# Warm matmuls moved and added between the transposes, kv and x steps of the first batch

## Chip, cores, metric

One core of a Trainium2 chip. The metric is the time of one execution on the device in microseconds. Executions of one kernel lie up to some 2 us apart here, so medians and means over several are compared, and, where it matters, single executions by the TensorE clock that each of them lists.

## The reference

Linear attention over 8 batches, 8 heads, 576 rows of 64, then a feed-forward layer with exact Gelu, all float32 at the border:

```python
q_s = softmax(q, axis=-1)            # over the 64 of a row
k_s = softmax(k, axis=2)             # over the 576 rows
kv  = einsum('bhsd,bhse->bhde', k_s, v)
x   = einsum('bhsd,bhde->bhse', q_s, kv)   # then heads joined: 4608 x 512
h   = x @ w_in                       # 512 -> 2048
out = gelu(h) @ w_out                # 2048 -> 512
```

## The kernel before

The kernel treats each batch (512 of its 576 rows) as transposes of q, kv, x, h and y; the rests of all batches come last. Matmul operands are bf16. While the first data come in, TensorE (PE in the profile) runs matmuls on zeros, so that its clock is up when real work starts: in the trace of this kernel their starts lie 0.43 us apart until the clock comes up at 3.98 us, then 0.216 us, and the first transposes start at 9.33. These are called warm matmuls here.

```python
def warm(n):
    ps = psum_y.tile([128, DM], FP32, tag="y")
    for i in range(n):
        nc.tensor.matmul(ps, zeros[:, 0:128], zeros, start=True, stop=True)
...
setup_tiles()
warm(27)
table(AF.Exp)
exp_q(0, parts=2)
exp_k(0, parts=2)
norm_q(0, 0, 2)                       # POOL
norm_q(0, 1, 2, nc.vector)
tp_mm(0, 0)                           # 8 transposes
tp_evac(0, 0, "s")
table(AF.Gelu)
warm(2)
cast_v(0, 0)
for hp in range(1, HP):
    cast_v(0, hp, nc.gpsimd)
cast_wi(0, wi[0], "p")
cast_wi(1, wi[1], "p")
tp_mm(0, 1)                           # 8 transposes
for hp, pool, tag in ((0, psum_y, "y"), (1, psum_y, "y"), (2, psum_a, "a"), (3, psum_h, "h")):
    x_tile(0, hp, pool, tag)
kv_mm(0, 0)
kv_norm(0, 0, 1)                      # DVE
tp_evac(0, 1)
x_mm(0, 0)
...
h_phase(0, {0: [lambda: cast_wi(2, wi[2], "v")],   # third block of w_in, cast in 4 row blocks
            2: [lambda: cast_wi(3, wi[3], "v")],
            ...}, groups={0: 2})
```

In `h_phase` the tiles of h are computed one after another (tiles 0 and 1 interleaved), four matmuls each, one per row block of w_in. The third block of w_in holds tiles 4 to 7.

The softmax here doesn't subtract the row's maximum and nothing guards it: scores larger than these inputs give would overflow.

## Time and profile before

| | before |
|---|---|
| time, first three executions | 283.36, 283.38, 284.02 us |
| profiled execution | 283.92 us (span 282.1), listed clock 0.991 |
| PE busy | 97% of the span |
| half clock in the trace | 14.22 to 17.63 us, and after the last matmul |

The listed clock is the mean over the span. In this trace the stretch of 3.41 us at half clock takes 0.5 x 3.41 / 282 = 0.006 off it, and the idle end of the kernel, at half clock from 280.46 us, 0.003 more: 0.991. The clocks listed in this study fall into two groups, 0.988 to 0.993 and 0.997 or more (one execution at 0.853 aside); the two traces with a dip list 0.991, the nine without one and without a cold start 0.998 or more. So an execution that lists 0.997 or more is counted here as one without a dip inside, and one at 0.993 or less as one with.

### The profile page before, as it was taken

The page shows a single profiled execution, that of the slowest core. Times are in us where ns is not written, and L with a number is a line of the kernel's source. Part 1 is how long each engine was busy: PE and PEld are TensorE (multiplying, and loading weights), DVE is VectorE, ACT ScalarE, POOL GpSimd, SP SyncE. Part 2 cuts the span into 40 slices and gives each one's busy share as a digit, 9 for nine tenths or more (in the row PEclk, how much of TensorE's full clock was granted, in tenths as well). Part 3 has the DMA queues.
Part 4 walks back from the last instruction along what each step waited for, and adds up shares of the span by engine and source line. Part 5 has one row for each costly group of instructions (what it writes and reads, how often), then busy time and mean ns, then how long its engine had stood idle before and what let it go on. Part 6 is the DMA issues. An engine that isn't in the chain of part 4 may idle for free.

```text
span 282.1 us, 4576 instructions
## 1 busy us (share of the span) xinstructions
PE 273.1 (97%) x1933; PEld 126.3 (45%) x1933; DVE 101.8 (36%) x149; ACT 156.7 (56%) x242; POOL 32.8 (12%) x25
## 2 busy tenths in 40 slices
PE   8699999999999899999999999999999999999994
PEld 3334454444444344444444444444444444444443
DVE  2766586309760470075006510562006200230021
ACT  5756753689467914693468436862683364036400
POOL 0530040002020050005000500050005000000000
PEclk9979999999999999999999999999999999999998
DMA  7999999951629429911991179226601500120033
GB/s 233 382 404 428 401 402 406 401 223 55 136 83 349 163 80 249 379 41 39 221 369 47 74 198 346 89 77 164 136 0 74 149 2 0 74 77 0 2 74 74
DMA packets 44852, 50.09 MB, mean 178 GB/s; under 512 B 20385, under 2 KB 29857, under 8 KB 44577
## 3 DMA queue, kind: packets, MB, share of 16 engines
q1 hardware_dynamic: 44544, 49.68, 51.9%
q8 instruction: 15, 0.25, 0.4%
q10 hardware_dynamic: 288, 0.13, 0.2%
q14 instruction: 5, 0.03, 0.1%
HBM read 36.70 MB, written 9.44 MB: 164 GB/s over the span
## 4 chain that ended last, share of the span: by engine, by line
PE 84%; DMA 7%; DVE 3%; ACT 2%; SPq 1%; issue 1%; POOL 0%; ACTq 0%
PE ps L294 40%; PE ps L304 39%; DMA f<-in_v_dram 6%; PE kv L165 2%; PE ps L250 2%; DMA f<-in_q_dram 1%; PE ps L326 1%; DVE v_aug L144 1%; DVE qsum L195 1%; ACT ek L137 1%; ACT e L132 1%; DVE e L197 1%; SPq L230 0%; DVE y_sb L311 0%; ACT L132 0%
## 5 line engine op out<-in xcount | busy, mean ns | idle before, releaser
L294 PE MATMUL ps<-xT,wi_bf 128*128 128x512 bf16 x576 | 127.2, 382 | 0.0
L304 PE MATMUL ps<-wo_bf,g 128*128 128x512 bf16 x560 | 124.4, 379 | 1.3 <-DVE y_sb L311 1.3
L299 ACT ACTIVATE g<-ps 128x512 bf16<-128x512 f32 x144 | 85.6, 597 | 68.6 <-PE ps L294 68.6
L294 PEld LDWEIGHTS <-wi_bf 128*128 128x128 bf16 x576 | 56.6, 99 | 69.2 <-issue 1.9
L304 PEld LDWEIGHTS <-g 128*128 128x128 bf16 x560 | 54.0, 98 | 65.7 <-issue 2.0
L311 DVE COPY y_sb<-ps 128x512 f32<-128x512 f32 x35 | 23.8, 683 | 74.5 <-PE ps L304 74.1
L197 POOL TENSOR_TENSOR e<-e,recq 128x2048 bf16<-128x2048 bf16 (+1 forms) x9 | 25.7, 2855 | 179.1 <-DVE recq L196 146.9
L144 DVE CAST v_aug<-f 128x576 bf16<-128x576 f32 x26 | 17.9, 745 | 57.3 <-DMA f<-in_v_dram 57.2
L276 ACT CAST xT<-ps 128x512 bf16<-128x512 f32 x19 | 10.2, 588 | 31.9 <-PE ps L250 22.3
L195 DVE TENSOR_REDUCE qsum<-e 128x16 f32<-128x1024 bf16 (+1 forms) x13 | 21.0, 1618 | 15.6 <-ACT e L132 15.6
L132 ACT ACTIVATE e<-f 128x512 bf16<-128x512 f32 (+1 forms) x42 | 20.5, 556 | 1.2 <-DMA f<-in_q_dram 1.1
L137 ACT ACTIVATE ek<-f 128x2304 bf16<-128x2304 f32 (+1 forms) x10 | 17.2, 1730 | 2.4 <-DMA f<-in_k_dram 2.4
L274 DVE CAST xT<-ps 128x512 bf16<-128x512 f32 x15 | 9.7, 686 | 15.5 <-PE ps L250 12.7
L78 ACT ACT_TABLE_LOAD x9 | 11.5, 1283 | 2.8 <-issue 2.6
L404 PE MATMUL ps<-zeros 128*128 128x512 bf16 x29 | 8.0, 435 | 1.2 <-DVE scr L73 1.2
L132 ACT ACT_TABLE_LOAD x7 | 9.0, 1283 | 0.1
L165 PEld LDWEIGHTS <-ek 64*64 64x64 bf16 x576 | 6.6, 105 | 3.1 <-issue 1.2
L378 DVE CAST wi_bf<-w 128x512 bf16<-128x512 f32 (+1 forms) x8 | 7.1, 903 | 2.1 <-DMA w<-in_moe_w_in_dram 2.0
L165 PE MATMUL kv<-v_aug,ek 64*64 64x65 bf16 x576 | 7.1, 193 | 0.7 <-POOL v_aug L144 0.4
L397 DVE CAST wo_bf<-w 128x2048 bf16<-128x2048 f32 (+1 forms) x5 | 5.1, 1013 | 4.5 <-DMA w<-in_moe_w_out_dram 4.4
L197 DVE TENSOR_TENSOR e<-e,recq 128x1024 bf16<-128x1024 bf16 x4 | 6.3, 1586 | 0.1
L250 PE MATMUL ps<-qT,kvc 64*64 64x512 bf16 x60 | 5.2, 406 | 1.2 <-DVE kvc L176 1.2
(29 smaller groups left out, 40.5 us busy)
## 6 DMA issues: line engine op xcount, KB each, us to landing
out_dram<-y_sb SPq DMA_DIRECT2D x32, 256.0 KB, 2.3
f<-in_k_dram SPq DMA_DIRECT2D x6, 1152.0 KB, 10.0
f<-in_v_dram SPq DMA_DIRECT2D x6, 1152.0 KB, 11.6
f<-in_q_dram SPq DMA_DIRECT2D x6, 1024.0 KB, 7.5
w<-in_moe_w_in_dram SPq DMA_DIRECT2D x6, 512.0 KB, 8.4
f<-in_k_dram SPq DMA_DIRECT2D x4, 576.0 KB, 10.1
f<-in_v_dram SPq DMA_DIRECT2D x8, 288.0 KB, 8.1
f<-in_q_dram SPq DMA_DIRECT2D x4, 512.0 KB, 8.6
```

Source lines behind the costliest of these rows:

```text
L78: nc.scalar.activation(out=scr[:, 1:2], in_=scr[:, 0:1], func=func)
L132: nc.scalar.activation(out=dst[:, i], in_=src[:, u], func=AF.Exp)
L137: nc.scalar.activation(out=ek[b % 2][:, i:i + n], in_=st[b]["kf"][:, i:i + n].rearrange("p x (n d) -> p x n d", n=NS), func=AF.Exp,)
L144: eng.tensor_copy(out=v_aug[b % 2][:, hp, :, 0:D], in_=st[b]["vf"][:, hp, :].rearrange("p (n d) -> p n d", n=NS),)
L165: nc.tensor.matmul(ps[c, i, half, 0:D + 1], ek[b % 2][pr, hp, n, :], v_aug[b % 2][pr, hp, n, 0:D + 1], start=(n == 0), stop=(n == NS - 1),)
L195: nc.vector.reduce_sum(out=qsum, in_=eq[:, :, hs, :], axis=AX.X)
L197: eng.tensor_tensor(out=eq[:, :, hs, :], in0=eq[:, :, hs, :], in1=recq.unsqueeze(3).to_broadcast([128, J, w, D]), op=ALU.mult,)
L250: nc.tensor.matmul(ps[c, :], kvc[b][pr, hp, :], st[b]["qT"][pr, :, hp, :], start=True, stop=True,)
L294: nc.tensor.matmul(ps, wi_bf[:, dm, t * 128:(t + 1) * 128], xT[:, dm, :], start=(dm == 0), stop=(dm == NDM - 1),)
L299: nc.scalar.activation(out=g[:, t, :], in_=ps, func=AF.Gelu)
L304: nc.tensor.matmul(ps, st[c]["g"][:, t, j * 128:(j + 1) * 128], wo_bf[:, t, :], start=(t == 0), stop=(t == NDF - 1),)
L311: nc.vector.tensor_copy(out=y_sb, in_=ps)
```

## The change

Intent: to keep PE busy enough around the first kv and x step for the clock to stay up, without delaying them. Two warm matmuls move from the opening to behind the second transposes, and four new ones, on zeros, write the x tiles before x does.

```diff
+    def warm_x():
+        for r in range(2):
+            for i in range(2):
+                pr = slice(r * 64, r * 64 + 64)
+                c = slice((r ^ i) * 64, (r ^ i) * 64 + 64)
+                nc.tensor.matmul(
+                    st[0][f"x{i}"][c, :], zeros[pr, 0:64], zeros[pr, :], start=True, stop=True,
+                )
...
-    warm(27)
+    warm(25)
...
     tp_mm(0, 1)
+    warm(2)
     for hp, pool, tag in ((0, psum_y, "y"), ...
...
     tp_evac(0, 1)
+    warm_x()
     x_mm(0, 0)
```

## The prediction

The windows of the clock, here and below, are the stretches of 3.41 us that its steps mark in the traces: before the change it first comes up at 3.98 us, and its steps at 14.22, 17.63 and 280.46 us lie 3, 4 and 81 times 3.41 us after that.

> **What bounds the kernel now.** I read the page first, for which engine is full; then the windows view in small slices, for where TensorE's clock drops; then the chain of waits over the first 40 us, for what the changed code waits on; then the timeline of 8 to 20 us and of 42 to 47 us, for how early the later work could start.
>
> ```profile
> PE 273.1 (97%) x1933; PEld 126.3 (45%) x1933; DVE 101.8 (36%) x149; ACT 156.7 (56%) x242; POOL 32.8 (12%) x25
> ...
> PEclk9979999999999999999999999999999999999998
> DMA  7999999951629429911991179226601500120033
> ```
>
> TensorE (PE) is busy for 97% of the span, so after the start the kernel is a stream of matmuls. The third digit of PEclk, 14 to 21 us, shows a stretch at a lower clock. The DMA row shows that the transfers are full for the first 56 us. Both matter here. In slices of 0.1 us the clock reads 0.59 in 14.20:14.30 and 0.84 in 17.60:17.70, so it fell to half at 14.22 us and came back at 17.63 us: a dip of 3.41 us. The only other drop is at the end, in the slice 280.00:280.50 (0.96), so at 280.46. From 17.63 to 280.46 are 77.0 times 3.41, and counted back the same steps fall on 14.22, 10.81 and 7.39 us. I therefore cut the start into those stretches (columns: PE, PEld, DVE, ACT, POOL busy, clock, DMA share, GB/s):
>
> ```profile
> 7.39:10.81 3.42, 2.52 (x22) 1.21 (x21) 3.28 (x4) 2.25 (x3) 1.88 (x1) 1.00 1.01 377
> 10.81:14.22 3.41, 1.86 (x82) 1.19 (x79) 1.73 (x6) 3.28 (x6) 2.24 (x4) 1.00 1.08 392
> 14.22:17.63 3.41, 3.21 (x11) 1.12 (x12) 2.48 (x5) 0.84 (x2) 2.20 (x4) 0.50 1.06 402
> ...
> 277.05:280.46 3.41, 1.33 (x19) 1.03 (x17) 0.85 (x2) 0.00 (x0) 0.00 (x0) 1.00 0.55 135
> ```
>
> PE was busy for 74% of the first stretch and kept its clock. It was busy for 55% of the second and 39% of the last, and after each of those the clock was halved for the next stretch. The third stretch, at half clock, was full, and the clock came back. The bar lies, for this run, between 55% and 74%. The timeline shows where the holes of the second stretch are:
>
> ```profile
> 10.50 0.61 PE L211 MATMUL ps<-identity,e 128*128 128x128 bf16 x8
> ...
> 11.23 0.22 PE L165 MATMUL kv<-v_aug,ek 64*64 64x65 bf16 x2
> ...
> 11.88 0.47 PE L165 MATMUL kv<-v_aug,ek 64*64 64x65 bf16 x34 [0.43 <-POOL v_aug L144]
> ...
> 12.95 0.41 PE L250 MATMUL ps<-qT,kvc 64*64 64x512 bf16 x4 [0.60 <-DVE kvc L176]
> ...
> 14.42 0.64 PE L250 MATMUL ps<-qT,kvc 64*64 64x512 bf16 x4 [0.60 <-DVE kvc L176]
> ```
>
> The holes are 11.45 to 11.88 (the cast of v on POOL, itself waiting for v from DMA until 11.11), 12.35 to 12.95 and 13.85 to 14.42 (the normalisation on DVE). The change fills the first two.
>
> [...]
>
> **The change part by part.**
> 1. The opening burst goes from 27 to 25 matmuls. At full clock a 128x512 matmul takes 0.216 us (four per Gelu; their starts lie 0.86 us apart). So the burst ends at about 8.11 and not 8.54 us. The transposes wait for POOL until 9.33 either way: 0 us on the path. The stretch 7.39:10.81 loses 0.43 of its 2.52 us: 2.09, 61%.
> 2. Two such matmuls after the second transposes: 11.11 to 11.54, then the two early kv matmuls (0.22) to 11.76. The other kv matmuls are released at 11.88. 0 us on the path, 0.12 to spare.
> 3. Four 64x64 matmuls of 512 columns before x: like the x step's 0.41 us, two at a time. They run 12.38 to 12.80; x is released at 12.95. 0 us on the path, 0.15 to spare. The PSUM tiles of the y pool trade places, but earlier users there are PE's own warm matmuls, so no wait across engines appears.
> 4. The stretch 10.81:14.22 then holds 1.86 + 0.43 + 0.41 = 2.70 us, 79%, above the 74% that kept the clock. I expect no dip at this phase of the windows.
>
> **What the missing dip is worth.** At the start of h: the second x step takes 0.43 in place of 0.58 us to the next start, so the h matmuls begin at 14.85 and not 15.00. With all 64 at 0.216 us they would end 1.4 us earlier than now. But weights and v come from a full DMA and do not come earlier:
>
> ```profile
> 18.92 0.62 DVE L378 CAST wi_bf<-w 128x512 bf16<-128x512 f32 x1 [0.85 <-DMA w<-in_moe_w_in_dram]
> ...
> 42.76 0.75 DVE L144 CAST v_aug<-f 128x576 bf16<-128x576 f32 x1 [0.36 <-DMA f<-in_v_dram]
> ```
>
> The first line is the last quarter of the third block of w_in, ready at 19.54. Matmul number 19 (from 0: its fifth tile, fourth row block) needs it. Now it runs at about 30.11 - 45 x 0.216 = 20.39; without the dip it would want to at 14.85 + 19 x 0.216 = 18.95. It waits 0.6 us, starts at 19.57, and the y matmuls begin at 19.57 + 9.72 = 29.29 in place of 30.11: 0.82 us left. The later weight casts are in time (the tightest, rows 2 and 3 of the fourth block, is done at 22.51 and wanted at 22.8).
> The second line is v of batch 1, whose cast ends at 43.51. DVE must do it before it normalises the first kv of batch 1: 0.17 and 0.29 us with their gaps, released to PE at 44.06. PE's x step, now at 44.56, would want 43.74. It waits 0.32 us, and 0.82 - 0.32 = 0.50 us are left. After 46 us no later wait is near; the rest moves as a block. So a run with this dip should gain **0.5 us**, of a raw 1.4.
>
> **Was the median with the dip?** The three times lie at 283.36, 283.38 and 284.02, and the profiled execution, which had the dip, took 283.92. A difference of 0.5 to 0.6 us is just what I work out for dip against no dip. So I lean to this: the two fast runs had none, with the windows lying otherwise, and the median is already that of a run without. Then the change removes only the slow half of the executions, and the median hardly moves.
>
> **The rivals.**
> - (a) All runs before had the dip, DMA noise makes the spread, and the change takes it away: 283.38 - 0.5 = 282.9 us. For it: the profiled run has it. Against: the two groups of times. Chance 0.3.
> - (b) The median was already without it: 283.3 to 283.4. Chance 0.4.
> - (c) No DMA ceiling, the whole 1.4 us is gained: 282.0. Against: the DMA share over 1.0 in every stretch from 4 to 44 us, and DVE waiting for w_in. Chance 0.05.
> - (d) The dip moves. The two matmuls taken from the burst leave 7.39:10.81 at 61%, inside the unknown 55 to 74%[...]. Then the half clock comes at 10.81, the fillers last twice as long (0.86 us) and delay kv and x by some 0.3 us each: kv, x and fillers on the path double and about 1 to 1.3 us are lost before h, of which the DMA ceiling again hides part. Time 283.4 to 284.2. Chance 0.25.
>
> **Range and chances.** 0.3 x 282.9 + 0.4 x 283.35 + 0.05 x 282.0 + 0.25 x 283.8 = 283.26; I say **283.2 us**, with a range of **282.6 to 283.9** (the low end a little under (a), the high end inside (d)). 2% is 5.7 us, and the whole dip costs at most half of 3.41 us = 1.7 us: within 2% is all but certain, 0.98, with 0.01 on each side.
>
> **What would show it.** Right: clock 1.00 from 4 to 280 us; the fillers at 11.1 and 12.4 with no wait of their own; kv still released by POOL at 11.88 and x by DVE at 12.95; h from 14.85; a new wait of h matmuls for the w_in cast near 19 us of about 0.6 us; y from 29.3; a new wait of x in batch 1 near 43.8 us of about 0.3 us. Wrong: a dip at 10.81 or 14.22 all the same (my bar or my count of busy time is wrong); no wait at 19 us and y at 28.7 (the ceiling is not there); x of batch 0 later than 13.0 (fillers on the path); or a time below 282.6, which would need the full gain.

## The result, and the profile after

283.40 us in the median of six executions (282.53 to 284.14), against 283.37 us for six of the kernel before (282.91 to 284.02). The ratio is 0.9997, with a 95% interval of 0.9975 to 1.0019: the same. (A ratio here is the mean time of one kernel's fast runs over that of the other's of the same rounds, so not quite the ratio of the medians.) The profiled execution took 283.44 us, span 281.7, and lists a clock of 1.000. The outputs are right.

The page of the changed kernel, the lines that answer to those of before:

```profile
PE 272.7 (97%) x1937; PEld 126.0 (45%) x1937; DVE 101.8 (36%) x149; ACT 156.8 (56%) x242; POOL 32.9 (12%) x25
...
PEclk9999999999999999999999999999999999999999
DMA  7999999952439329901990179226501500210033
```

The low stretch at 14 to 21 us is gone; the other rows shown here differ little. The windows view of the changed kernel, cut where its own clock windows lie (columns as in the prediction). Here the clock came up at 5.29 us and not at 3.98, so the windows lie 1.3 us later against the kernel (the clock record of this trace stays full for 276.48 us, again 81.0 times 3.41):

```profile
8.70:12.12 3.42, 2.38 (x23) 1.34 (x23) 2.48 (x2) 3.06 (x3) 1.11 (x2) 1.00 1.04 390
12.12:15.53 3.41, 2.17 (x84) 1.16 (x84) 1.68 (x6) 2.85 (x6) 2.61 (x5) 1.00 1.08 396
```

Both stretches, PE busy for 70% and 64%, kept the clock. Because the windows lie elsewhere, this one trace does not show yet that the new matmuls did it. The timeline of PE in the changed kernel (start, length, line and operands, idle before and its cause):

```profile
11.01 0.59 PE L404 MATMUL ps<-zeros 128*128 128x512 bf16 x2
11.72 0.22 PE L165 MATMUL kv<-v_aug,ek 64*64 64x65 bf16 x2
12.38 0.47 PE L165 MATMUL kv<-v_aug,ek 64*64 64x65 bf16 x34 [0.44 <-POOL v_aug L144]
12.66 0.41 PE L412 MATMUL ps<-zeros 64*64 64x512 bf16 x4
13.45 0.41 PE L250 MATMUL ps<-qT,kvc 64*64 64x512 bf16 x4 [0.38 <-DVE kvc L176]
...
15.27 4.27 PE L294 MATMUL ps<-xT,wi_bf 128*128 128x512 bf16 x19
19.77 9.89 PE L294 MATMUL ps<-xT,wi_bf 128*128 128x512 bf16 x45 [0.24 <-DVE wi_bf L378]
29.50 10.52 PE L304 MATMUL ps<-wo_bf,g 128*128 128x512 bf16 x48
...
44.14 0.41 PE L250 MATMUL ps<-qT,kvc 64*64 64x512 bf16 x4
```

The fillers (L404 at 11.01, L412 at 12.66) lie in the holes: kv is still released by POOL's cast and x by DVE's normalisation. All of it is 0.5 us later than before, because v of the first batch landed 0.5 us later in this execution (POOL's cast begins at 11.66 and not at 11.16). The h matmuls therefore begin at 15.27 and not at 14.85. The new wait is where it was expected, in front of matmul 19, for the cast of w_in: 19.77 - 15.27 - 19 x 0.216 = 0.40 us. (The idle time of 0.24 in the view is shorter, because the ends of matmuls are modelled; starts are safer.) The y matmuls start at 29.50, 0.61 us earlier than before, x of batch 1 at 44.14, 0.42 us earlier, and the span is 0.4 us shorter. So between these two traces 0.4 us were gained; between the medians nothing was.

### The profile page after: what moved, and what is told of

It reads as the page before. It is cut to its first block, busy times and chain, and to the rows that moved or that the text cites. A ratio compares the mean times of both kernels' runs of the same rounds, so it can differ in the third digit from the quotient of the medians.

```text
span 281.7 us, 4584 instructions
## 1 busy us (share of the span) xinstructions
PE 272.7 (97%) x1937; PEld 126.0 (45%) x1937; DVE 101.8 (36%) x149; ACT 156.8 (56%) x242; POOL 32.9 (12%) x25
## 4 chain that ended last, share of the span: by engine, by line
PE 73%; DMA 18%; DVE 4%; ACT 2%; SPq 1%; issue 1%; ACTq 0%
PE ps L294 34%; PE ps L304 34%; DMA f<-in_v_dram 9%; DMA f<-in_q_dram 4%; DMA w<-in_moe_w_in_dram 3%; DMA touch<-in_moe_w_in_dram 2%; PE kv L165 2%; PE ps L250 1%; PE ps L326 1%; DVE v_aug L144 1%; DVE qsum L195 1%; ACT ek L137 1%; ACT e L132 1%; DVE e L197 1%; SPq L230 0%
## 5 line engine op out<-in xcount | busy, mean ns | idle before, releaser
L404 PE MATMUL ps<-zeros 128*128 128x512 bf16 x29 | 8.8, 462 | 1.2 <-DVE scr L73 1.2
```

## The experiments

Two theories were to be told apart from the start. **Mine:** the clock's windows lie elsewhere against the kernel in other executions; before the change only some executions have the dip, which is worth about 0.5 us after a ceiling that DMA sets; the median execution had none. **The rivals:** every execution before had it (a); no ceiling, a dip costs its full 1.4 us (c); the change moves the dip (d).

Each kernel got six executions, one of them profiled, beside eleven of the kernel before on the same chip.

### Which executions dip: the kernel before, the changed one, and two parts

No edit in the first two. `e1_no_mid` is the kernel before without its `warm(2)` between the transposes; `e1_burst25` has only the first part of the change:

```diff
# e1_no_mid                      # e1_burst25
     table(AF.Gelu)              -    warm(27)
-    warm(2)                     +    warm(25)
```

> The kernel before, unchanged, for the clock that each execution lists. My theory ([...]the dip costs 0.5 us net): some executions list about 0.991 to 0.994 (dip) and others 0.997 or more (none), and those with the dip are 0.4 to 0.7 us slower. Rival (a), every execution has the dip: all list 0.994 or less, and the spread of the times has no tie to the clock.

> The changed kernel, unchanged. My theory: every execution lists 0.997 or more, since the fillers keep the clock at every position of the windows; median equal to that of the dipless executions of the kernel before. Rival (d), the dip moves for some positions of the windows: some executions list under 0.995.

> The kernel before without its two warm matmuls between the transposes, so with less PE work in front of kv (0.43 us less in the stretch 7.4 to 10.8 us). My theory: the dip comes in more of the executions than in the kernel before, and the median is 0.2 to 0.5 us above it, because the ceiling set by DMA hides the rest. If DMA set no ceiling, dipped executions would be 1.4 us slower.

> Only the first part of the change: the opening burst 25 and not 27, nothing added. If the shorter burst can itself bring the dip (rival d), dips are more frequent here than in the kernel before; if not, as frequent. Either way within 0.3 us of the kernel before in the median.

Measured: `e1_before_again` 283.53 us in the median, three of six executions at 0.991 or 0.992 (283.69, 283.71, 283.79 us), three at 0.997 or more (282.50, 283.12, 283.37). `e1_after_again` 283.14 us, all six at 0.998 or more, ratio to the kernel before 1.000 (0.998 to 1.002). `e1_burst25` 283.48 us, no dip in six. `e1_no_mid` 282.94 us, one dip in the five fast ones; its sixth execution is of another kind: it lists 0.853 and took 321.57 us, where the others took 282.13 to 283.79. It is left out of all comparisons; what else ran on the chip is not known.

So executions differ, as my theory says, and rival (a) is out. (Only two of the executions with a dip have a trace, `before` and `e1_before_again`, and both dip at 14.2 us; for the others the listed clock tells that they dipped, and not where.) Each row is all fast executions with a listed clock; the kernel before is pooled over three chips, and its dips were 4 of 17, 6 of 11 and 4 of 11 there:

| kernel | executions | with the dip | mean without, us | mean with, us |
|---|---|---|---|---|
| before | 39 | 14 | 283.07 | 283.93 |
| changed (with the first six) | 18 | 0 | 283.21 | |
| burst 25 only | 6 | 0 | 283.34 | |
| no warm matmuls between transposes | 5 | 1 | 282.61 | 283.79 |
| lighter, before | 6 | 2 | 281.88 | 283.33 and 285.31 |
| lighter, changed without `warm_x` | 6 | 1 | 281.84 | 283.88 |
| lighter, changed | 6 | 0 | 282.03 | |
| two waits later (with all fillers) | 12 | 1 | 282.96 | 284.11 |

With all fillers 1 of 36 executions dipped; without any of the change 16 of 45. The dip of the kernel before costs 283.93 - 283.07 = 0.86 us in the mean (0.71, 0.94 and 0.86 on the three chips). The dipless executions of the two kernels agree within their scatter (a standard deviation of 0.55 us before, 0.53 after). The single parts have too few executions to be told from each other by counts: `e1_no_mid`, expected to dip more often, did so in 1 of 5, and its median was no slower. That expectation is not borne out. Nor do the counts exclude that the shorter burst alone lowers the chance of a dip (0 of 6 in `e1_burst25`).

### Lifting the ceiling: half the bytes of w_in

```diff
+            m = n if i < 2 else n // 2
-            nc.sync.dma_start(out=w[:, c:c + d, 0:n], in_=src[:, c:c + d])
+            nc.sync.dma_start(out=w[:, c:c + d, 0:m], in_=src[:, c:c + d, 0:m])
...                                  # the cast: the loaded half twice
-                nc.vector.tensor_copy(out=o[:, c:c + d], in_=w[:, c:c + d])
+                for z in range(0, r, m // 128):
+                    nc.vector.tensor_copy(out=o[:, c:c + d, z:z + m // 128], in_=w[:, c:c + d])
```

> The changed kernel with half of the bytes of the last three w_in blocks (1.5 MB less; the loaded half is cast twice; the result is wrong on purpose). It lifts the DMA ceiling without touching the clock. My theory (h waits 0.2 to 0.6 us for w_in and x of batch 1 waits 0.3 us for v): 0.5 to 0.9 us faster than the changed kernel. Rival (c), no ceiling: no difference over 0.2 us.

Measured: 282.00 us in the median, all six between 281.90 and 282.27 (wrong result). That is 1.2 us below the mean of the changed kernel, somewhat more than expected, and the scatter shrinks from 1.6 us (the first six of the changed kernel) to 0.4. PE no longer waits for DVE's casts of w_in. So the ceiling is there, rival (c) is out, and the scatter of executions without the dip comes for the most part from when the loads land. The traces of the unlightened changed kernel agree: the wait in front of h's matmuls for the cast of w_in was 0.24 us of idle time in the first, and in that of `e1_after_again` (its waits of PE):

```profile
PE ps L294 <- DVE wi_bf L378: 1.2, 2, 0.9
```

There y began only at 29.88 us, though the clock was full. In the trace of `e3_after` there was no such wait, and y began at 28.89:

```profile
15.06 13.99 PE L294 MATMUL ps<-xT,wi_bf 128*128 128x512 bf16 x62
28.89 10.52 PE L304 MATMUL ps<-wo_bf,g 128*128 128x512 bf16 x47
```

This run happened to give the trace that was missing: its clock came up at 3.93 us, as in the kernel before (3.98), so its windows lie as there. The windows view of `e2_light`:

```profile
7.34:10.75 3.41, 1.99 (x18) 0.91 (x17) 3.34 (x4) 2.32 (x3) 1.90 (x1) 1.00 1.02 378
10.75:14.17 3.42, 2.53 (x90) 1.36 (x87) 1.79 (x6) 3.24 (x6) 2.28 (x4) 1.00 1.07 390
14.17:17.58 3.41, 3.23 (x17) 1.49 (x19) 2.80 (x9) 2.03 (x5) 2.23 (x4) 1.00 1.09 380
```

At the position where the kernel before had 1.86 us of PE work in the second stretch and lost its clock for the third, this one has 2.53 us and keeps it. PE's instructions are those of the changed kernel, and w_in plays no part in PE's work before h begins at 14.64 us, so in this stretch the fillers are what differs. The profile of `e1_before_again` fell on this position too (clock up at 3.97) and dipped again, at 14.21 us, after a stretch with 1.87 us of PE work:

```profile
10.79:14.21 3.42, 1.87 (x82) 1.18 (x79) 1.75 (x6) 3.29 (x6) 2.26 (x4) 1.00 1.07 389
14.21:17.62 3.41, 3.22 (x11) 1.13 (x12) 2.54 (x5) 0.82 (x2) 2.18 (x4) 0.50 1.04 375
```

The first stretch of `e2_light` also answers rival (d) for this position: the shorter burst leaves it at 1.99 us, 58%, and that was enough.

### A certain cold start, with and without the ceiling

`e2_cold` is the changed kernel with one warm matmul in all; `e2_cold_light` has the lighter w_in too (wrong result):

```diff
-    warm(25)
+    warm(1)
...                # and both warm(2) and warm_x() taken out
```

> The changed kernel without any warm matmul (one is left in the opening), so that h starts at half clock in every execution: a certain, longer dip. Lost before the ceiling: about 1 us on the transposes, kv and x and 1.3 to 2.9 us on h, some 3 us. My theory: the ceiling hides 0.8 us of it, so 1.5 to 2.8 us slower than the changed kernel, clock listed 0.98 to 0.99. No ceiling: 2.5 to 4 us slower.

> No warm matmuls and the lighter w_in together (wrong result on purpose). With the ceiling gone, the whole loss of the cold start should show: against the lighter kernel 2.5 to 4 us slower, that is 0.5 to 1 us more than the cold kernel loses against the changed one. If there is no ceiling, the two losses are equal within 0.3 us.

Measured: `e2_cold` 284.43 us in the median, mean 284.72; `e2_cold_light` 284.54 us, mean 284.60. Against the five dipless executions of the kernel before (283.05) the cold start costs 1.67 us; against the changed kernel's 18 executions (283.21) 1.5. With the lighter w_in it costs 284.60 - 282.03 = 2.57 us. So 0.9 to 1.1 us are hidden by the ceiling, at the upper end of what was expected (0.5 to 1). The length of the cold stretch depends on where the windows lie (until 18.27 us in the one profile, 20.64 us in the other), so with six executions each this difference has a standard error of some 0.4 us. One part of the expectation was wrong: the listed clock is 0.997 to 1.000 and not 0.98 to 0.99, because the record of the clock begins only when it first comes up, and the cold start lies before that (the windows view lists 1.00 there, though h's matmuls start 0.43 us apart).

### The raw cost of the dip, and half of the fillers

`e3_light_before` is the kernel before with the lighter w_in; `e3_light_no_warm_x` is `e2_light` without the `warm_x()` call.

> The kernel before with half of the bytes of the last three w_in blocks (wrong result on purpose), so with the DMA ceiling away and its noise too; the changed kernel in this form took 281.9 to 282.3 us in all six executions. My theory: dipped executions (clock listed 0.991 to 0.994) are 1.2 to 1.7 us slower than dipless ones, the raw cost of the dip, and dipless ones take 282.0 us as the changed kernel does. If the dip cost only 0.5 to 0.9 us here too, the ceiling would not be what hides it.

> The lighter changed kernel without the four matmuls before x (wrong result on purpose): only the two warm matmuls moved from the opening to behind the second transposes. Dipless executions 282.0 us. If the moved two are enough, no execution has the dip; if the four before x are needed, some have it (0.991 to 0.994, some 1.4 us slower).

Measured: `e3_light_before`, four executions without the dip at 281.67 to 282.22 us, as the changed kernel in this form (and 1.28 us below the dipless ones of the kernel before, 283.16), one at 283.33 (clock 0.992) and one at 285.31 (0.988). The first is 1.45 us above the mean of the dipless ones, as the worked-out raw cost of 1.4 us. The other is 3.4 us above it. Its clock lacks 0.012, more than one stretch of 3.41 us and the idle end took together in the trace of `before` (0.009) and as much as two stretches take; no trace of it exists, so that it had two is worked out and not seen. `e3_light_no_warm_x`: 281.76 to 282.06 us in five executions and 283.88 us (0.992) in one. That one lies 2.04 us above the others' mean, more than the 1.7 us that the prediction took for the most that a dip can cost; it has no trace, so where it dipped is not known. So the raw cost rests on two executions, 1.45 and 2.04 us. The two moved matmuls alone do not keep the clock in every execution; whether they lower the chance, one in six cannot say.

### Putting the two waits later

```diff
-    }, groups={0: 2})           # h of batch 0
+    }, groups={0: 2, 4: 2})
...
-    cast_v(1, 3)                # after the transposes of batch 1
     ...
     kv_mm(1, 0)
     kv_norm(1, 0, 1)
+    cast_v(1, 3)
```

> The changed kernel with its two DMA waits put later: tiles 4 and 5 of h of batch 0 interleaved, so that the late quarter of w_in is wanted 3 matmuls later, and the last cast of v of batch 1 behind the first normalisation. No byte and no matmul differs, the result is right. My theory: the waits at 19 and 43.8 us shrink or go, 0.3 to 0.8 us faster than the changed kernel. If the waits cost nothing: same within 0.2 us.

> The version with the two DMA waits put later, again and beside the changed kernel on one chip. Mine: 0.1 to 0.4 us below the changed kernel in the mean of dipless executions (its trace showed the first wait moved to 22.5 us rather than gone).

> The changed kernel again, to count dips beside the kernel before on the same chip. Mine: at most one execution under 0.995, where the kernel before has about a third; mean 0.2 to 0.4 us below that of the kernel before.

Measured: `e2_two_waits` 282.93 us (mean 283.08, one dip at 284.11), `e3_two_waits` 282.77 us (mean 283.02), and on the same chip as the latter `e3_after` 283.14 us (mean 283.04). Between the means on one chip that is 0.02 us, with a scatter of 0.6 us in each: the expected 0.1 to 0.8 is not seen. Six executions each can't exclude a few tenths; the table's dipless means, over several chips, lie 0.25 us apart. The trace shows that the wait moved. The waits of PE's weight loads (PEld), and a line of PE's timeline, in `e2_two_waits`:

```profile
PEld L294 <- DVE wi_bf L378: 1.6, 3, 0.7
```

```profile
22.55 6.65 PE L294 MATMUL ps<-xT,wi_bf 128*128 128x512 bf16 x29 [0.19 <-DVE wi_bf L378]
```

By the starts of its matmuls PE waited 0.28 us for the third block of w_in and 0.35 us for the fourth, at 22.5 us. Here the wait that DMA sets was not removed by changing the order in which PE asks; the next bytes were late too. No version with a right result beats both kernels by more than the noise.

`e3_after` itself: six executions at 0.998 or more, mean 283.04, against 283.47 for the eleven of the kernel before, of which four dipped. The ratio is 0.9988 (0.996 to 1.0016), in the expected direction and size (0.2 to 0.4 us) but within noise.

## Why the prediction was right, point by point

- **The number: right, but it decides little.** 283.40 lies within 282.6 to 283.9, and so would rivals (a), (b) and much of (d) have done. What tells them apart are the listed clocks and the traces.
- **The dip comes from too little PE work in one window, and the fillers end it: right.** At the same position of the windows 1.86 and 1.87 us lost the clock and 2.53 us kept it; over all executions 16 dips in 45 without the change, 1 in 36 with it. The worked-out fill was 2.70 us. The prediction put its bar between 55 and 74%; in the three traces at this position the stretches with PE busy for 55% lost the clock, and the one with 58% kept it. More than that is not shown. The longest gap of PE did not decide: the stretch of `before` that lost the clock has none over 0.60 us (1.55 us in all), and the one of `e2_light` with 58% has a single one of 1.31 us (1.42 in all) and kept it. Regaining the clock took more in two traces: counted back from where the clock came up in `e2_cold_light` (20.64 us), two stretches at half clock with PE busy for 2.70 and 2.58 us, 79% and 76%, did not bring it up, while 3.19 us, 94%, did in `e2_cold`.
- **The fillers cost nothing on the path: right.** kv stays released by POOL and x by DVE, in every trace of the changed kernel that was read. (Where v landed early, as in `e1_after_again`, the two early kv matmuls run up to the release, so that the view lists no wait there.)
- **The median before was already without the dip (b): right.** 25 of 39 executions had none. So the change removes the slower third: 14/39 x 0.86 = 0.31 us in the mean, and next to nothing in the median. The scatter of the loads (0.55 us) covers it.
- **The ceiling set by DMA: right in kind.** In the trace after, the wait in front of matmul 19 was 0.40 us (predicted 0.6), y began at 29.50 (29.29), and x of batch 1 waited 0.19 us (0.32): from the start of kv it took 1.57 us to reach x, against 1.38 us in the trace of `e1_after_again`, which had no such wait. The first was shorter because h had begun 0.42 us later than predicted (v landed 0.5 us late, and from the second x step to h it took 0.35 us and not the 0.43 of the prediction), and the weight was ready only 0.20 us later. In sum 0.42 us were gained at that point, for a predicted 0.50. But the wait is not there in every execution: the trace of `e3_after` shows none and y from 28.89, which is near the prediction's own sign that the ceiling is not there (28.7), and that of `e1_after_again` shows more, with y from 29.88.
- **The worth of a dip, 0.50 us: too small.** In the mean of executions it was 0.86 us, of a raw 1.45 or 2.04. The term that was probably mis-sized is what the ceiling hides: 0.9 us in the sum, against 1.45 - 0.86 = 0.6 us with the one execution whose raw cost fits the worked-out 1.4 (with the other it would be 1.2, so the size is not settled). It was taken from the landing times of one trace, and these move by half a microsecond from one execution to the next. The cold start, a longer loss, had 0.9 to 1.1 us hidden.
- **The dip moves to 10.81 us (d), given a chance of 0.25: not seen.** The stretch that lost the two matmuls kept the clock at 58%. The one dip with all fillers, and the one of `e3_light_no_warm_x`, have no trace, so for these two (d) is not excluded.

How the windows lie changes from execution to execution: in the profiles at full clock with an opening burst of 25 or 27 the clock first came up anywhere from 3.93 to 6.08 us.

What stays open: how much each of the two groups of fillers, and the shorter burst, does alone, and where the one dip in 36 executions with all fillers fell.

## What to carry to other kernels

Before working on a dip of the clock that one profile shows, count in how many executions it comes: the listed mean clock of each execution is enough, and the profiled one may be of the minority. Fillers in PE's waits were free here because they ended before what releases the next real matmul (at 13.07 us, with x starting at 13.45, in the trace after), and what they could win was bounded by the next ceiling: PE then waited for loads (0.40 and 0.19 us in that trace), which took back a good part. To see a few tenths of a microsecond under such noise, take the ceiling away in a test kernel (here half the bytes of a weight), where the same effect stands alone.
